# Storing three second-level factors in the first group, and loading the quarters of the rest two sets ahead

## The chip, the cores and the metric

The kernel runs on one core of a Trainium2 chip. The metric is the device time of one execution in microseconds; lower is better. Several runs are taken and the median is used. The profile comes from one further execution, of which a trace of every instruction was kept; its time is given beside its span (first to last instruction).

## What is computed

An attention with a decaying state, over 12 blocks of 64 tokens, feeds a two-layer map with the activation h - tanh(h):

```python
B, H, S, D = (4, 8, 768, 64)
for b in range(nb):                       # blocks of 64 tokens
    intra = einsum('bhic,bhjc->bhij', qb, kb) * Dmask
    out[:, :, sl] = einsum('bhij,bhjd->bhid', intra, vb) + einsum('bhid,bhde->bhie', qb * lam_pow, kv_state)
    kv_state = lam_block * kv_state + einsum('bhsd,bhse->bhde', kb * rev_pow, vb)
x = out.transpose(0, 2, 1, 3).reshape(3072, 512)
h = x @ w_in                              # w_in  512 x 2048
return (h - tanh(h)) @ w_out              # w_out 2048 x 512
```

All arithmetic is in 32-bit floats, and the result is 3072 x 512.

## The kernel before

**Groups.** The tokens are worked off in six groups (`g` = 0 to 5) of 512 rows: 128 positions of each of the four batches. For each group the attention gives x transposed (`xt`), the "up" product makes the hidden values g, and the "down" product makes the output.

**Group 0** is computed plainly (`up_plain`, `down_plain`), while the weights come in. Each raw block is rounded (`round_block`: ACT L239 and L241, VectorE L242 to L248). `down_plain(kt)` goes through the eight row blocks `kt` of w_out. For each of them `sums_out(kt)` forms, from the four blocks B11, B12, B21, B22 of w_out, the sums T1, T2, T4, T3 of a Strassen-Winograd product (L221 to L224), and stores the seven factors B11, B21, B22, T1, T2, T4, T3 into the DRAM tensor `factors` (L226, L227, issued by POOL). The weight tile `wt` (pool `wst`, two buffers) is filled again two `kt` later, by L241 first. Quarter `kt // 2` and row half `kt % 2` say where a row block belongs at the second level.

**Groups 1 to 5** use the seven products instead of eight, in both layers. `up(g, u, n)` is product n of column block u; its four accumulation banks are y (two, by the parity of u), z and w. z takes the products 5, 7 and 3, so product 5 of the next u can overwrite it only after VectorE has read it for product 3 (L419), and product 3 only after it has been read for product 7 (L414). In `down`, products 1 and 2 are done at one level (L501), products 4, 5, 6, 7 and 3 at two levels (`down_twice`, L539): each is again split in seven, and for this each of the five factors needs seven second-level factors, in the DRAM tensor `fine`: its blocks b11, b21, b22 and the sums t1, t2, t3, t4 of its four quarters.

**How `fine` is made.** This is done in group 1, in five turns among the 28 products of "up". `load_quarters(n)` loads the four quarters of one factor from `factors` (L444: 256 KB each, in pieces of 512 bytes), and `factors_twice(n)` forms four sums on VectorE (L459) and stores seven tiles to `fine` (L461). `turns` gives the count of products after which each turn comes. The quarters live in the ring `wb` of seven buffers, which the factor blocks of "down" use too (`piece`, L470 and L473, up to seven blocks ahead). The sums live in four buffers with the tag `sums`, three of them used by a turn.

**The order of work.** The instructions of each engine are put in order by a planner, in which what is ready first, and then what is written first, goes first; a sum marked `keep_in_program_order` stays behind what was written before it on its engine. Each engine then runs its instructions strictly in that order. Almost all transfers that concern weights, factors and outputs are issued by POOL; the loads of q, k and v are issued by SP, among them the small block loads of groups 2 to 5 (16 KB each, L136). Pools `qpool`, `wst` and `stage` are closed after group 0, and the pool `late` (ring `wb`, `sums`) takes their memory. Pool `o` has four buffers, for outputs: `ob` of group 0 (L601, stored at L602), later the products of "down".

Of the kernel before, what the change touches and what calls it, by code (L numbers as in the profile page):

```python
# [9 lines left out]
F32 = mybir.dt.float32  # L10
# [13 lines left out]
def kernel(  # L24
# [31 lines left out]
    nc = tc.nc  # L56
# [8 lines left out]
    NU = DFF // 512  # L65
# [11 lines left out]
    opool = ctx.enter_context(tc.tile_pool(name="opool", bufs=4))  # L77
# [6 lines left out]
    dram = ctx.enter_context(tc.tile_pool(name="dram", bufs=1, space=bass.MemoryType.DRAM))  # L84
# [32 lines left out]
    raw, late = {}, {}  # L117
# [49 lines left out]

    NX = 7
    factors = dram.tile([NX, 128, KH, 256], F32, name="factors")
    w_in_u = moe_w_in.rearrange("k (a n) -> k a n", a=2)  # L170
    blocks = [("in", u, i) for u in range(NU) for i in range(KI)] + [("out", kt, a) for kt in range(KH)
                                                                    for a in range(2)]
# [45 lines left out]
    def sums_out(kt):  # L218
        wt = pair[kt]
        b11, b12, b21, b22, t1, t2, t4, t3 = (wt[:, x] for x in range(8))  # L220
        nc.vector.tensor_tensor(t1, b12, b11, op=AL.subtract)  # L221
        nc.vector.tensor_tensor(t2, b22, t1, op=AL.subtract)
        nc.vector.tensor_tensor(t3, b22, b12, op=AL.subtract)
        nc.vector.tensor_tensor(t4, b21, t2, op=AL.subtract)  # L224
        f = factors[:].rearrange("x p k c -> p x k c")
        nc.gpsimd.dma_start(out=f[:, 0:1, kt, :], in_=wt[:, 0:1, :])  # L226
        nc.gpsimd.dma_start(out=f[:, 1:NX, kt, :], in_=wt[:, 2:8, :])  # L227

    def round_block(w, raw64):


        word = raw64.rearrange("p a n -> p (a n)").bitcast(U32).rearrange("p (n w) -> p n w", w=2)
        wordf = raw64.rearrange("p a n -> p (a n)").bitcast(F32).rearrange("p (n w) -> p n w", w=2)
        lo, hi = word[:, :, 0], word[:, :, 1]
        w = w.rearrange("p a n -> p (a n)")
        wb, wi = w.bitcast(U32), w.bitcast(I32)

        r = stage.tile([128, 512], I32, name="r", tag="r", bufs=2)
        nc.scalar.activation(r, lo, AF.Copy, scale=2.0 ** -29)  # L239

        nc.scalar.activation(w, wordf[:, :, 1], AF.Abs)  # L241
        nc.vector.tensor_scalar(out=w, in0=w, scalar1=CLAMP, scalar2=None, op0=AL.max)  # L242

        nc.vector.tensor_scalar(out=wb, in0=wb, scalar1=3, scalar2=0x3FFFFFF8, op0=AL.logical_shift_left,
                                op1=AL.bitwise_and)
        nc.vector.scalar_tensor_tensor(out=wb, in0=hi, scalar=0xC0000000, in1=wb, op0=AL.bitwise_and,
                                       op1=AL.bitwise_or)
        nc.vector.tensor_tensor(wi, wi, r, op=AL.add)  # L248
# [109 lines left out]
    def attention(g):  # L358
        pieces = [[(fn, g, bs) for fn in (att_transpose, att_scores, att_out, att_state)] for bs in ((0, 1), (2, 3))]
        pieces[1].append((att_sums, g, None))  # L360
        return pieces


    FACT = {1: ("A11", "B11"), 2: ("A12", "B21"), 3: ("S4", "B22"), 4: ("A22", "T4"), 5: ("S1", "T1"),
            6: ("S2", "T2"), 7: ("S3", "T3")}
    XAT = {"B11": 0, "B21": 1, "B22": 2, "T1": 3, "T2": 4, "T4": 5, "T3": 6}
# [57 lines left out]

    SUB = (1, 2, 6, 5, 7, 3, 4)
    TWICE = (4, 5, 6, 7, 3)

    fine = dram.tile([len(TWICE), len(SUB), 128, NU, 128], F32, name="fine")  # L430
    HIDAT = {"A11": 11, "A12": 21, "A22": 22, "S1": "S1", "S2": 11, "S3": 12, "S4": 21}
    RING = 7

    def twice(g, n):
        return n in TWICE and not (g == NG - 1 and n == 3)

    stream = [(g, n, x) for g in range(1, NG) for n in (1, 2, 4, 5, 6, 7, 3)
              for x in (SUB if twice(g, n) else range(NU))]
    sent = {"n": 0}

    def factor_block(t, x, i, j):

        src = factors[x].rearrange("p (u m) c -> p u m c", m=2)
        nc.gpsimd.dma_start(out=t, in_=src[:, :, i, ts(j, 128)])  # L444

    quarters = {}

    def load_quarters(n):
        for i in range(2):
            for j in range(2):  # L450
                quarters[n, i, j] = late["pool"].tile([128, NU, 128], F32, name="wq", tag="wb", bufs=RING)
                factor_block(quarters[n, i, j], XAT[FACT[n][1]], i, j)

    def factors_twice(n):

        b11, b12, b21, b22 = (quarters.pop((n, i, j)) for i in range(2) for j in range(2))
        t1, t2, t4 = (late["pool"].tile([128, NU, 128], F32, name=f"wt{x}", tag="sums", bufs=4) for x in (1, 2, 4))
        for dst, x, y in ((t1, b12, b11), (t2, b22, t1), (b12, b22, b12), (t4, b21, t2)):
            tc.keep_in_program_order(nc.vector.tensor_tensor(dst, x, y, op=AL.subtract))  # L459
        for i, t in enumerate((b11, b21, t2, t1, b12, b22, t4)):  # L460
            nc.gpsimd.dma_start(out=fine[TWICE.index(n), i], in_=t)  # L461

    def piece(g, n, x):

        i = stream.index((g, n, x))
        while sent["n"] < min(i + RING, len(stream)):
            g_, n_, x_ = stream[sent["n"]]
            t = late["pool"].tile([128, 2, 256], F32, name="wb", tag="wb", bufs=RING)
            if twice(g_, n_):
                nc.gpsimd.dma_start(out=t.rearrange("p m c -> p (m c)"),  # L470
                                    in_=fine[TWICE.index(n_), SUB.index(x_)].rearrange("p u c -> p (u c)"))
            else:
# [20 lines left out]
    def down(g, n):  # L493

        t, first = product_bank(("down", g), n)
        a = hidden(g, HIDAT[FACT[n][0]])
        for u in range(NU):
            wb = piece(g, n, u)
            for m in range(2):
                for kt in range(2):  # L500
                    nc.tensor.matmul(out=t[:, m, :], lhsT=a[:, u, kt, ts(m, 128)], rhs=wb[:, kt, :],  # L501
                                     start=first and u == 0 and m == 0 and kt == 0, stop=u == NU - 1 and kt == 1,
                                     skip_group_check=True)
        t = t.rearrange("q m c -> q (m c)")
        if n == 1:
            res[g, 1] = otile("q1")
            nc.scalar.activation(res[g, 1], t, AF.Copy)
        else:
            o11 = late["pool"].tile([128, 512], F32, name="o11", tag="o11", bufs=1)
            nc.vector.tensor_tensor(o11, res[g, 1], t, op=AL.add)  # L510
            store(g, 11, o11)
            sums_once(g, 11, "S1", 11)
# [6 lines left out]
    def sums_twice(g, n):  # L519
        a11, a12, a21, a22 = quarter(g, n)  # L520
        s1, s2 = (late["pool"].tile([128, NU, 128], F32, name=f"s{x}", tag="sums", bufs=4) for x in (1, 2))
        nc.vector.tensor_tensor(s1, a21, a22, op=AL.add)
        nc.vector.tensor_tensor(s2, s1, a11, op=AL.subtract)
        nc.vector.tensor_tensor(a21, a11, a21, op=AL.subtract)
        low[g, n] = (s1, s2)
# [79 lines left out]
    def run(pieces):  # L605
        for fn, *args in pieces:
            fn(*args)
# [31 lines left out]
    early.close()  # L639
    late["pool"] = ctx.enter_context(tc.tile_pool(name="late", bufs=1))  # L640

    turns, made = (4, 9, 14, 19, 23), []
    load_quarters(TWICE[0])
    up(1, 0, 1)
    for g in range(1, NG):
        last = g == NG - 1
        p0, p1 = attention(g + 1) if not last else ([], [])
        for u in range(NU):
            for n in (2, 6, 5, 7, 1, 4, 3):
                if n != 1:  # L650
                    up(g, u, n)
                elif u + 1 < NU:
                    up(g, u + 1, 1)
                else:
                    down(g, 1)
                if g == 1:
                    made.append(n)
                    if len(made) in turns:
                        t = turns.index(len(made))
                        factors_twice(TWICE[t])  # L660
                        if t + 1 < len(TWICE):
                            load_quarters(TWICE[t + 1])
            if not last and u > 1:
                run(p0[u - 2:u - 1])
        sums_twice(g, 4)
        down(g, 2)
        run(p0[2:])
        sums_twice(g, 5)
        down_twice(g, 4, "z")
        run(p1[0:1])  # L670
        sums_once(g, 21, 21, 11)
        sums_twice(g, 6)
        down_twice(g, 5, "w")
        run(p1[1:2])
        sums_twice(g, 7)
        down_twice(g, 6, "z")
        if not last:
            sums_twice(g, 3)
        run(p1[2:])
        down_twice(g, 7, "w")  # L680
        if not last:
            up(g + 1, 0, 1)
            down_twice(g, 3, "z")
        else:
            down_end(g)
# [30 lines left out]
```

## Time and profile before

| | |
|---|---|
| three runs | 697.58, 697.76, 699.11 us; median 697.76 |
| the profiled execution | 696.26 us, span 694.5 us |
| instructions | 12442 |
| mean granted TensorE clock | 0.990 |
| DMA | 123.27 MB, mean 177 GB/s |
| POOL's queue (q0) | 91.77 MB, 40.8% of 16 engines' span |
| SP's queue (q1) | 30.71 MB, 22.8% |
| quarters loaded (L444) | 20 of 256 KB, 759 ns of POOL each, 5.6 us to landing |
| second-level factors stored (L461) | 20 quarters and 15 sums of 256 KB, 540 to 557 ns of POOL each |
| sums of quarters (L459) | 20 of 0.68 us |

Parts of the span, from the starts of TensorE's instructions: down_plain from 83.7 to 154.6 us; "up" of group 1 from 154.6; `down(1, 1)` at 215.4; the two-level products of group 1 from 241.1; the last matmuls end at 691.7. A busy time is the time in which an engine was at work, and DMA share is the mean busy share of the 16 DMA engines. In the timeline and the waits, what stands after the arrow is what the waiting instruction was released by.

### The profile page before, as it was taken

What the parts mean: (1) busy time and instruction counts of PE and PEld (TensorE: products, weight loads), DVE (VectorE), ACT (ScalarE), POOL (GpSimd) and SP (SyncE); (2) the same over time, 40 slices, a digit from 0 to 9 for tenths busy, and PEclk for the clock granted to TensorE, in tenths of its full rate; (3) what the DMA queues carried; (4) which work ended last, traced back from release to release, by engine and by line L of the source; (5) the groups of instructions that cost most, each with busy time, mean ns of one, the idle gap of its engine ahead of it and who ended that gap; (6) DMA issues with size and microseconds to landing.
All of it is one profiled execution on the core that took longest, in us unless ns stands there. A gap on an engine that the chain in (4) does not pass through costs nothing.

```text
span 694.5 us, 12442 instructions
## 1 busy us (share of the span) xinstructions
PE 669.3 (96%) x4688; PEld 578.5 (83%) x4688; DVE 449.1 (65%) x786; ACT 195.0 (28%) x392; POOL 184.9 (27%) x328
## 2 busy tenths in 40 slices
PE   6899999999796999999999999999999999999998
PEld 5688855558575899988899988899888899988898
DVE  3797766995366886347787356778346786345653
ACT  2664433323120112232112233122233122233120
POOL 0001212124664244100244200243400144400262
PEclk9999999999898999999999999999999999999999
DMA  9879868468988798544598820687820376600385
GB/s 190 217 215 228 278 174 261 143 156 255 286 261 245 216 273 242 161 82 84 134 266 243 227 54 14 136 247 217 254 46 2 90 214 211 214 1 0 96 289 178
DMA packets 160475, 123.27 MB, mean 177 GB/s; under 512 B 133536, under 2 KB 133920, under 8 KB 160416
## 3 DMA queue, kind: packets, MB, share of 16 engines
q0 software_dynamic: 27552, 91.77, 40.8%
q1 hardware_dynamic: 132720, 30.71, 22.8%
q8 instruction: 37, 0.61, 0.4%
q14 instruction: 22, 0.18, 0.1%
q10 hardware_dynamic: 144, 0.00, 0.0%
HBM read 99.62 MB, written 22.81 MB: 176 GB/s over the span
## 4 chain that ended last, share of the span: by engine, by line
PE 79%; DMA 9%; issue 7%; POOL 3%; DVE 1%; ACT 1%; SPq 0%; POOLq 0%
PE y L393 16%; PE y L539 11%; PE zw L539 8%; PE z L393 8%; PE h L581 8%; PE y L501 5%; PE w L501 5%; DMA wq<-factors 4%; PE op L597 4%; PE w L393 4%; PE sp L291 3%; PE op L342 2%; DMA wb<-fine 2%; DMA raw<-in_moe_w_in_dram 1%; PE op L336 1%
## 5 line engine op out<-in xcount | busy, mean ns | idle before, releaser
L470 POOL DMA_DIRECT2D wb<-fine x168 | 90.3, 538 | 141.7 <-PE y L539 55.5
L473 POOL DMA_DIRECT2D wb<-factors x44 | 23.9, 544 | 187.1 <-PE y L501 176.9
L393 PE MATMUL y<-xt,w 128*128 128x256 f32 x320 | 73.2, 380 | 0.0
L393 PEld LDWEIGHTS y<-xt,w 128*128 128x128 f32 x320 | 60.5, 190 | 8.6 <-issue 0.5
L401 ACT ACTIVATE th<-g 128x512 f32<-128x512 f32 x60 | 37.7, 630 | 99.6 <-DVE g L419 42.9
L539 PE MATMUL y<-wb,g 128*128 128x128 f32 x456 | 61.3, 278 | 0.3 <-ACT r L542 0.3
L542 ACT ACTIVATE q<-y 128x128 f32<-128x128 f32 x96 | 26.6, 277 | 121.2 <-PE y L539 120.3
L402 DVE TENSOR_TENSOR g<-g,th 128x512 f32<-128x512 f32 x60 | 41.4, 690 | 27.9 <-ACT th L401 27.7
L539 PEld LDWEIGHTS y<-wb,g 128*128 128x128 f32 x456 | 55.7, 192 | 2.0 <-issue 0.8
L597 PE MATMUL op<-wt,g 128*128 128x512 f32 x128 | 56.5, 596 | 0.0
L581 PE MATMUL h<-xt,w 128*128 128x256 f32 x256 | 56.1, 381 | 0.0
L581 PEld LDWEIGHTS h<-xt,w 128*128 128x128 f32 x256 | 48.4, 190 | 7.2 <-issue 0.3
L597 PEld LDWEIGHTS op<-wt,g 128*128 128x128 f32 x128 | 23.9, 190 | 27.7 <-issue 27.0
L393 PE MATMUL z<-xt,ws 128*128 128x256 f32 x160 | 39.7, 393 | 4.6 <-DVE g L414 4.6
L501 PE MATMUL y<-wb,g 128*128 128x256 f32 x160 | 37.4, 393 | 6.4 <-DMA fine<-wq 6.4
L414 DVE TENSOR_TENSOR g<-g,z 128x512 f32<-128x512 f32 x20 | 13.7, 686 | 45.2 <-ACT g L413 45.2
L501 PEld LDWEIGHTS y<-wb,g 128*128 128x128 f32 x160 | 31.4, 197 | 11.2 <-issue 6.8
L539 PE MATMUL zw<-wb,g 128*128 128x128 f32 x304 | 40.2, 276 | 0.0
L393 PEld LDWEIGHTS z<-xt,ws 128*128 128x128 f32 x160 | 31.4, 197 | 9.5 <-DVE g L414 5.0
L393 PE MATMUL z<-tt,ws 128*128 128x256 f32 x160 | 37.9, 380 | 1.4 <-DVE g L419 1.4
L393 PE MATMUL w<-xt,w 128*128 128x256 f32 x160 | 38.8, 387 | 0.0
L393 PE MATMUL y<-tt,w 128*128 128x256 f32 x160 | 38.4, 382 | 0.0
(119 smaller groups left out, 1222.9 us busy)
## 6 DMA issues: line engine op xcount, KB each, us to landing
wb<-fine POOLq DMA_DIRECT2D x168, 256.0 KB, 3.9
wb<-factors POOLq DMA_DIRECT2D x44, 256.0 KB, 5.1
raw<-in_moe_w_out_dram POOLq DMA_DIRECT2D x16, 512.0 KB, 4.9
v_nat<-in_v_dram SPq DMA_DIRECT2D x24, 256.0 KB, 5.1
factors<-wt POOLq DMA_DIRECT2D x8, 768.0 KB, 5.5
k_nat<-in_k_dram SPq DMA_DIRECT2D x20, 256.0 KB, 5.4
wq<-factors POOLq DMA_DIRECT2D x20, 256.0 KB, 5.6
fine<-wq POOLq DMA_DIRECT2D x20, 256.0 KB, 4.0
```

The source lines that it names most:

```text
L291: nc.tensor.matmul(out=sp[j][:, p, :], lhsT=kt[ts(j, 64), p, :], rhs=qt[ts(j, 64), p, :], start=True, stop=True)
L342: nc.tensor.matmul(out=dst(n, p, j), lhsT=vn[:, 2 * p + j, :], rhs=ss[:, j, p, :], start=g == 0 and n == 0 and p % 2 == 0, stop=n == 1 and ...
L393: nc.tensor.matmul(out=t[:, m, :], lhsT=wt[:, kt, ts(m, 128)], rhs=x[:, kt, :], start=first and m == 0 and kt == 0, stop=kt == 1, skip_gro ...
L401: nc.scalar.activation(th, src, AF.Tanh)
L402: nc.vector.tensor_tensor(dst(c), src, th, op=AL.subtract)
L470: nc.gpsimd.dma_start(out=t.rearrange("p m c -> p (m c)"), in_=fine[TWICE.index(n_), SUB.index(x_)].rearrange("p u c -> p (u c)"))
L473: nc.gpsimd.dma_start(out=t, in_=factors[XAT[FACT[n_][1]]][:, 2 * x_:2 * x_ + 2, :])
L501: nc.tensor.matmul(out=t[:, m, :], lhsT=a[:, u, kt, ts(m, 128)], rhs=wb[:, kt, :], start=first and u == 0 and m == 0 and kt == 0, stop=u = ...
L539: nc.tensor.matmul(out=dst, lhsT=a[:, u, :], rhs=wb[:, ts(u, 128)], start=x in (1, 2) and u == 0, stop=u == NU - 1, skip_group_check=True)
L542: nc.scalar.activation(keep, dst, AF.Copy)
L581: nc.tensor.matmul(out=hm[:, m, :], lhsT=w1[u][:, i, a, ts(m, 128)], rhs=xt[0, t][:, i, :], start=m == 0 and i == 0, stop=i == KI - 1, ski ...
L597: nc.tensor.matmul(out=obank[b], lhsT=g, rhs=wt[:, 2 * a:2 * a + 2, :], start=kt == 0 and a == 0, stop=kt == KH - 1 and a == 1)
```

## The change

Three things change.

1. `fine` is created early, and `sums_out(kt)` stores into it too. What it stores are quarters that need no second-level sum: of each of B22, T1, T2, T4 and T3 the quarter b11 (even `kt`), or b21 and b22 (odd `kt`). One store writes the same quarter of five factors: 128 partitions, 5 factors, 128 numbers each.
2. `factors_twice` stores only the four sums t1, t2, t3 (in place of b12) and t4, no longer b11, b21, b22.
3. The sets of quarters are numbered 0 to 4 in the order `MADE` (factors 4, 5, 6, 7, 3). Even sets stay in the ring `wb`, odd sets go into the four buffers of pool `o`. Sets 0 and 1 are loaded at the start, and set t + 2 after turn t. The turns come after 6, 11, 15, 20 and 24 products in place of 4, 9, 14, 19 and 23.

```diff
+    SUB = (1, 2, 6, 5, 7, 3, 4)
+    TWICE = (3, 5, 6, 4, 7)
+    fine = dram.tile([len(TWICE), len(SUB), 128, NU, 128], F32, name="fine")
...
         nc.gpsimd.dma_start(out=f[:, 0:1, kt, :], in_=wt[:, 0:1, :])
         nc.gpsimd.dma_start(out=f[:, 1:NX, kt, :], in_=wt[:, 2:8, :])
+
+        for x, j in ((1, 0),) if kt % 2 == 0 else ((2, 0), (3, 1)):
+            nc.gpsimd.dma_start(out=fine[:, SUB.index(x), :, kt // 2, :].rearrange("n p c -> p n c"),
+                                in_=wt[:, 3:8, ts(j, 128)])
...
-    def factor_block(t, x, i, j):
-
-        src = factors[x].rearrange("p (u m) c -> p u m c", m=2)
-        nc.gpsimd.dma_start(out=t, in_=src[:, :, i, ts(j, 128)])
-
+    MADE = (4, 5, 6, 7, 3)
     quarters = {}

-    def load_quarters(n):
+    def load_quarters(t):
+        src = factors[XAT[FACT[MADE[t]][1]]].rearrange("p (u m) c -> p u m c", m=2)
         for i in range(2):
             for j in range(2):
-                quarters[n, i, j] = late["pool"].tile([128, NU, 128], F32, name="wq", tag="wb", bufs=RING)
-                factor_block(quarters[n, i, j], XAT[FACT[n][1]], i, j)
-
-    def factors_twice(n):
-
-        b11, b12, b21, b22 = (quarters.pop((n, i, j)) for i in range(2) for j in range(2))
+                if t % 2 == 0:
+                    x = late["pool"].tile([128, NU, 128], F32, name="wq", tag="wb", bufs=RING)
+                else:
+                    x = opool.tile([128, NU, 128], F32, name="oq", tag="o")
+                nc.gpsimd.dma_start(out=x, in_=src[:, :, i, ts(j, 128)])
+                quarters[t, i, j] = x
+
+    def factors_twice(t):
+
+        b11, b12, b21, b22 = (quarters.pop((t, i, j)) for i in range(2) for j in range(2))
         t1, t2, t4 = (late["pool"].tile([128, NU, 128], F32, name=f"wt{x}", tag="sums", bufs=4) for x in (1, 2, 4))
         for dst, x, y in ((t1, b12, b11), (t2, b22, t1), (b12, b22, b12), (t4, b21, t2)):
             tc.keep_in_program_order(nc.vector.tensor_tensor(dst, x, y, op=AL.subtract))
-        for i, t in enumerate((b11, b21, t2, t1, b12, b22, t4)):
-            nc.gpsimd.dma_start(out=fine[TWICE.index(n), i], in_=t)
+        for x, src in ((5, t1), (6, t2), (7, b12), (4, t4)):
+            nc.gpsimd.dma_start(out=fine[TWICE.index(MADE[t]), SUB.index(x)], in_=src)
...
-    turns, made = (4, 9, 14, 19, 23), []
-    load_quarters(TWICE[0])
+    turns, made = (6, 11, 15, 20, 24), []
+    load_quarters(0)
+    load_quarters(1)
...
-                        factors_twice(TWICE[t])
-                        if t + 1 < len(TWICE):
-                            load_quarters(TWICE[t + 1])
+                        factors_twice(t)
+                        if t + 2 < len(MADE):
+                            load_quarters(t + 2)
```

More of the change, by code (lines that the diff above doesn't have):

```diff
@@ L423, in up @@
             nc.vector.tensor_tensor(dst(12), dst(11), dst(12), op=AL.subtract)
-    SUB = (1, 2, 6, 5, 7, 3, 4)
-    TWICE = (4, 5, 6, 7, 3)
-    fine = dram.tile([len(TWICE), len(SUB), 128, NU, 128], F32, name="fine")
     HIDAT = {"A11": 11, "A12": 21, "A22": 22, "S1": "S1", "S2": 11, "S3": 12, "S4": 21}
```

## The prediction

> **What bounds the kernel now.** I read the page's parts 1 and 2 first:
>
> ```profile
> PE 669.3 (96%) x4688; PEld 578.5 (83%) x4688; DVE 449.1 (65%) x786; ACT 195.0 (28%) x392; POOL 184.9 (27%) x328
> PEclk9999999999898999999999999999999999999999
> DMA  9879868468988798544598820687820376600385
> ```
>
> TensorE is busy for 96% of the span, so time can only come from its idle stretches or from slow matmuls. PEclk dips in slices 10 and 12 (about 174 and 208 us), the stretch in which group 1 makes its second-level factors. Next, the waits of TensorE alone; of its nine rows these belong to that stretch:
>
> ```profile
> PE y L501 <- DMA fine<-wq: 6.4, 1, 6.4
> ...
> PE z L393 <- DVE g L414: 4.6, 1, 4.6
> ...
> PE z L393 <- DVE g L419: 1.4, 1, 1.4
> ```
>
> They are 12.4 of the 22.3 us that the nine rows add up to. Then the timeline around them (start, length, engine, line, what it waited for):
>
> ```profile
> 181.00 0.69 DVE L459 TENSOR_TENSOR wt<-wq,wt 128x512 f32<-128x512 f32 x1 [6.85 <-DMA wq<-factors]
> ...
> 182.81 0.68 DVE L414 TENSOR_TENSOR g<-g,z 128x512 f32<-128x512 f32 x1
> ...
> 183.55 3.78 PE L393 MATMUL z<-xt,ws 128*128 128x256 f32 x8 [4.63 <-DVE g L414]
> ...
> 189.84 1.89 PE L393 MATMUL y<-tt,ws 128*128 128x256 f32 x8
> ...
> 209.31 0.55 POOL L473 DMA_DIRECT2D wb<-factors  x1 [0.42 <-DMA wq<-factors]
> ...
> 215.44 3.75 PE L501 MATMUL y<-wb,g 128*128 128x256 f32 x8 [6.39 <-DMA fine<-wq]
> ```
>
> A sum of quarters (L459) stands on VectorE until a quarter has landed; L414, which reads PSUM bank z, is queued behind it, and TensorE can't overwrite z. Later the first factor block of down(1,1) is issued only at 209.31, behind the last loads and stores of quarters. And eight matmuls after such a wait take 3.78 us instead of 1.89. The table by stretch (us, busy times, granted clock, DMA share, GB/s) says why, and how full the DMA engines are:
>
> ```profile
> 139.00:156.00 17.00, 17.00 (x89) 9.13 (x84) 15.86 (x30) 3.47 (x6) 4.05 (x6) 1.00 0.63 155
> 183.00:196.00 13.00, 12.45 (x45) 10.50 (x46) 8.40 (x14) 4.05 (x7) 7.32 (x12) 0.76 0.97 287
> 209.00:222.00 13.00, 6.61 (x21) 5.40 (x21) 8.11 (x14) 1.23 (x2) 5.21 (x10) 0.74 0.82 227
> ```
>
> **What the Trainium skill says.** "TensorE: Matmul & The Clock Gate", Part 1: after an idle window of about 3.4 us the array's clock is halved until it has been busy as long. The trace agrees: after 4.63 and 6.39 us idle the granted clock is 0.76 and 0.74, after 1.44 us the eight matmuls take 1.99 us. "DMA: Bandwidth & Descriptors", Specifications: full rate needs pieces of 512 B. The new stores and the quarter loads have just that; in 158 to 170 us, mostly quarter loads, the queue of POOL moves 2.65 MB in 12 us at 69.1% share, 320 GB/s per full share, and in 575 to 592, only 2 KB pieces, 3.51 MB in 17 us at 65.4%, 316. So 512 B cost nothing extra. The same page, Queues, rings and completion order: queues share the 16 engines in turn. In 183 to 196 the small block loads of SP take 17.1% and POOL's queue 79.6%.
>
> **What can be won.** TensorE's starts give it. Idle: 4.63 + 1.44 + 6.39 + 0.26 (before the block at 250.56) = 12.7 us. Slow restarts, by start-to-start against 1.73 for eight: 183.55 to 187.12 is 3.57 (+1.84), to 189.84 another 2.72 (+0.99), 205.26 to 209.05 +0.2, 215.44 to 218.99 is 3.55 (+1.82): 4.85. Together 17.5 us, all of it charged to the making of these factors.
>
> **The change, part by part.**
> - *Twelve stores more in the first group* (even kt one, odd two; 320 KB in 640 pieces). On POOL 512 pieces take 0.76 us (L444), 768 take 0.85 (L227): about 0.8 each, 9.6 us. They stand behind L227 of each kt, ahead of the next raw load (L179) or L226. POOL waits there for VectorE anyway: 2.24, 2.48, 6.14, 2.92 and 2.70 us after kt 2 to 6, so 0.8 or 1.6 fits. They hold the weight tile, whose next writer is L241 on ACT. From L227 to the L241 that refills the tile there are 9.0 us at worst (81.75 to 90.74, 99.34 to 108.40, 127.93 to 136.99); a store lands 2.5 + 5.1 = 7.6 us after L227 starts, up to 10.8 with the longest landing of the trace (8.3). Behind L241 are the other ACT work and the chain to L248, ready at 144.3 for a matmul at 147.75: 3.4 us of cover more. Cost 0; without the covers some 1.7 us each. DMA share there is 0.45 to 0.88; 3.93 MB at 320 GB/s are 12.3 us spread over 70.
> - *Fifteen stores less in group 1* (L461, three per turn): 8.4 us of POOL, as many bytes off the stretch at 0.82 to 0.97 share. They also freed late: a quarter's slot now opens with the sum that last reads it, except b12.
> - *Two sets ahead, odd sets in pool o.* A set is issued one turn before it is needed today, 6 to 8 us landing included; later, it has two turns, some 15 us. Set 1 goes where the outputs ob lie: their stores were issued by 159.2 and land in 4.3, so that set is issued by about 164 and is needed at about 178. For sets 2 to 4 the same count leaves 3 to 6 us.
> - *Turns at 6, 11, 15, 20, 24*: same 20 sums of 0.6 us. A product takes 1.73 us, so without waits turn k falls at 154.6 + 1.73 (k + 1): 166.7, 175.4, 182.3, 190.9, 197.8, and down(1,1) starts at 199.5 rather than 215.4.
> - *Queued behind a late sum*: on VectorE, L419 or L414 that free bank z; TensorE's next product in z stands behind them.
>
> **What remains.** (1) Turn 0: the stores of kt 7 (two, to 155.2) lie ahead of set 0 in the queue, and the late pool takes the memory of the weight tiles, so set 0 may have to wait for them. Set 0's last quarter landed near 166.3; 0.66 MB at 262 GB/s (80% of 325) is 2.5 us, the landing wait up to 2.2. So 168.5 to 171; three sums after it, then L419 by 171 to 173.6; TensorE wants z at 171.85. 0 to 1.7, I take 0.9. (2) down(1,1): from 152.7 POOL's queue must move before the first block: f 0.79, its two stores 0.66, ob 1.05, quarters 5.24, stores of four turns 4.19, the block 0.26: 12.2 MB, at 262 GB/s 46.5 us, to 199.2, needed at 199.5. The fourth block waits for turn 4's first sum, near 200 to 201. 0 to 2 us, I take 1.0. (3) Other short waits, 0 to 1: 0.4. Sum 2.3, none over 3.4 us, so no restart. Gain 17.5 - 2.3 = 15.2. The profiled execution (696.26, span 694.5 and 1.76 around it) becomes 681.1; the median of the runs is 1.5 above it, so 697.76 - 15.2 = 682.6.
>
> **Rivals.**
> - *The wait moves to the DMA engines.* POOL's queue got 2.65 MB in 12 us in one stretch (221 GB/s), 3.11 in 13 (239) in another: 12.2 MB then take 51 to 55 us, and down(1,1) waits 4 to 8 us with a restart of 1.8. For it: the shares of 0.9. Against it: those rates had POOL waiting in between. Won 17.5 - 8 to 10: 688 to 690. Chance 0.20.
> - *Turn 0 and its restart.* Set 0 held behind ob and the kt 7 stores for 4 us more: VectorE's queue stops, TensorE stands 4 to 5 us and restarts slowly (2.8): 17.5 - 7.5 - 1.4: about 689. Against it: ob's stores were in the queue before too. Chance 0.12.
> - *Slower: the buffers of the sums.* A turn takes three of four `sums` tiles, so its second sum waits for the store of the last turn's first to land. Turns lie 6.9 us apart once waits are gone, and stores queue behind up to eight loads (2.1 MB, 8 us). Bank z gives 1.7 us more. Up to 8.6 us of landing nothing is lost; each us above costs TensorE one at four turns. It takes (17.5 / 4) + 8.6 = 13 us to be slower; the longest landing seen is 8.3. With 14 to 15 us: 702 to 707. Chance 0.12.
> - *The change doesn't do what it says*: the planner issues the second set no earlier, or down's blocks still behind the last stores: 6.4 + 1.8 stay, and some of turn 1: near 697. Chance 0.04.
>
> **The numbers.** Forecast 682.6, chance 0.52, own range 680 to 686 (all of (1) to (3) at zero or at their most: 680.3 to 685.0). The two middle rivals reach 690, plus 2.5 for both in part: 679.8 to 692.5 leaves out the slower case, no change and a little more. Within 0.2% (1.4 us) is about what can't be told from no change. Faster 0.84 (0.52 + 0.20 + 0.12), same 0.03, slower 0.13.
>
> **What would show it.** Right: the rows of TensorE waiting for DMA and for L414 gone or under 2 us; PEclk without dips; down(1,1) starting near 200; turns at the times above; fine<-wq and fine<-oq together five, and twelve 320 KB stores to `fine` before 156 us, with L597 unbroken. Wrong: a new TensorE wait over 3.4 us in 154 to 225, ACT L241 waiting for a store, or VectorE's sums waiting for a store's landing.

## The result, and the profile after

The changed kernel takes 697.4 us (median of four runs, 696.2 to 698.1) where the kernel before takes 697.9 in the same comparison: a ratio of 0.9988, 95% interval 0.9970 to 1.0006. That is no difference. The forecast was 682.6. The profiled execution (697.4 us) has a span of 695.6 us, 1.1 more than before.

In the changed kernel the line numbers are some five to eight higher: L401 is the "up" product (before L393), L506 and L544 the "down" products (L501, L539), L464 the sums of quarters (L459), L279 the transposes of the q and k blocks (L271). L136, the block loads of SP, kept its number.

Rows of the page's part 2, after (the slices count from 0):

```profile
PE   6999999999979869999999999999999999999998
...
PEclk9999999999998979999999999999999999999999
DMA  9879869669967848544598740588820366600385
```

The clock's dip in slice 10 is gone. It dips in slices 12 and 14 now (209 to 226 and 243 to 261 us), and TensorE's busy share falls in 11, 13 and 14. The waits of TensorE in the changed kernel (total, times, longest):

```profile
PE zw L544 <- issue: 8.5, 1, 8.5
PE y L506 <- DVE g L410: 5.5, 1, 5.5
```

All three waits that the prediction set out to remove are gone: the two for L414 and L419, and the one ahead of down(1,1). Two new ones, of 14.0 us together, have come. TensorE's timeline in that stretch:

```profile
198.52 5.34 PE L506 MATMUL y<-wb,g 128*128 128x256 f32 x24
209.38 3.78 PE L506 MATMUL y<-wb,g 128*128 128x256 f32 x8 [5.51 <-DVE g L410]
...
249.66 2.04 PE L544 MATMUL zw<-wb,gS 128*128 128x128 f32 x8 [8.52 <-issue]
...
256.27 1.16 PE L544 MATMUL y<-wb,g 128*128 128x128 f32 x8
```

and the last of these products in the kernel before:

```profile
256.31 1.16 PE L539 MATMUL y<-wb,g 128*128 128x128 f32 x8
```

Down(1,1) starts at 198.52, where it started at 215.44, so 16.9 us had been won by then. At 230.16 the two-level products start, 10.9 us earlier than before. By 256.3 nothing of this is left: the product that starts there, at 256.27, started at 256.31 in the kernel before. VectorE's timeline names what it waited for:

```profile
198.71 0.70 DVE L279 STREAM_TRANSPOSE qt<-q_blk 128x512 f32<-128x512 f32 x1
207.43 0.71 DVE L279 STREAM_TRANSPOSE kt<-k_blk 128x512 f32<-128x512 f32 x1 [8.03 <-DMA q_blk<-in_q_dram]
...
247.68 0.71 DVE L279 STREAM_TRANSPOSE kt<-k_blk 128x512 f32<-128x512 f32 x1 [6.78 <-DMA k_blk<-in_k_dram]
```

Both waits are for k block tiles of the attention of group 2, loaded by SP. (The row at 207.43 names q_blk, but what the transpose reads is the k tile loaded just before it, issued until 205.92.) Behind the first stands L410, which the last quarter of down(1,1) needs; behind the second stands L549 (before L544), the subtraction that a product on bank zw needs. SP's queue in the changed kernel (start, length of 16 issues):

```profile
163.08 9.57 SPq L136 DMA_DIRECT2D q_blk<-in_q_dram  x16
...
196.67 9.25 SPq L136 DMA_DIRECT2D k_blk<-in_k_dram  x16
...
236.19 10.06 SPq L136 DMA_DIRECT2D k_blk<-in_k_dram  x16
```

and in the kernel before, with VectorE's last transpose of group 2:

```profile
157.10 10.11 SPq L136 DMA_DIRECT2D q_blk<-in_q_dram  x16
...
188.11 9.96 SPq L136 DMA_DIRECT2D k_blk<-in_k_dram  x16
...
233.00 8.23 SPq L136 DMA_DIRECT2D k_blk<-in_k_dram  x16
```
```profile
249.56 0.67 DVE L271 STREAM_TRANSPOSE kt<-k_blk 128x512 f32<-128x512 f32 x1
```

What SP waited for ahead of its first block load, before and then after, tells why the chain starts when it does (`wt` is the weight tile):

```profile
SPq L136 <- DVE wt L224: 6.8, 1, 6.8
SPq L136 <- DMA factors<-wt: 4.6, 1, 4.6
```
```profile
SPq L136 <- DMA factors<-wt: 10.1, 1, 10.1
SPq L136 <- DMA fine<-wt: 6.6, 2, 3.9
```

Before, it starts when the last store to `factors` has read the weight tile; after, the new stores to `fine` come last.

The reader should see a second chain beside the first one. The eight block tiles of group 2 are 128 loads on SP, issued one after the other, which takes 83 to 84 us in both kernels. Before, the fourth tile was out at 198.1 and VectorE took it at 210.9; the eighth was out at 241.2 and was taken at 249.6. The last three loads of these tiles landed at most 3.2 and 2.3 us after the start of their issue, so by about 200.8 and 243.1. That leaves some 10 and 6.5 us of slack, no more. After, this chain starts 6.0 us later, and TensorE arrives 11 to 17 us earlier.

The sum of TensorE's losses between "up" and 256 us then comes out nearly the same. After: 5.51 + 8.52 us idle and 5.3 us of slow matmuls behind these waits (209.38 to 215.39: 6.01 for sixteen of them where 3.46 is usual; 249.66 to 256.27: 6.6 where the kernel before took 3.9), 19.3 in all. Before it was 17.5, and group 0 ended 1.1 us later, 18.6 together; the two agree within 1 us.

### The profile page after: what moved, and what is told of

Same layout as the page of the kernel before. It is cut to its first block, busy times and chain, and to the rows that moved or that the text cites. A ratio compares the mean times of both kernels' runs of the same rounds, so it can differ in the third digit from the quotient of the medians.

```text
span 695.6 us, 12454 instructions
## 1 busy us (share of the span) xinstructions
PE 669.5 (96%) x4688; PEld 579.4 (83%) x4688; DVE 450.0 (65%) x786; ACT 194.7 (28%) x392; POOL 188.0 (27%) x325
## 4 chain that ended last, share of the span: by engine, by line
PE 79%; DMA 8%; issue 5%; SPq 2%; DVE 2%; POOL 2%; ACT 0%; POOLq 0%; DVEq 0%
PE y L401 16%; PE y L544 11%; PE z L401 8%; PE h L586 8%; PE zw L544 8%; PE w L506 5%; PE op L602 5%; PE y L506 5%; PE w L401 4%; PE sp L299 3%; DMA q_blk<-in_q_dram 3%; SPq L136 2%; PE op L350 2%; DMA wb<-fine 2%; PE tp L284 1%
## 5 line engine op out<-in xcount | busy, mean ns | idle before, releaser
L401 PE MATMUL y<-xt,w 128*128 128x256 f32 x320 | 73.2, 379 | 0.0
L401 PEld LDWEIGHTS y<-xt,w 128*128 128x128 f32 x320 | 60.5, 190 | 8.5 <-issue 0.5
L544 PE MATMUL y<-wb,g 128*128 128x128 f32 x456 | 61.3, 278 | 0.0
L410 DVE TENSOR_TENSOR g<-g,th 128x512 f32<-128x512 f32 x60 | 41.4, 689 | 27.5 <-ACT th L409 27.2
L544 PEld LDWEIGHTS y<-wb,g 128*128 128x128 f32 x456 | 55.7, 192 | 1.5 <-issue 0.3
L602 PE MATMUL op<-wt,g 128*128 128x512 f32 x128 | 56.5, 595 | 0.0
L602 PEld LDWEIGHTS op<-wt,g 128*128 128x128 f32 x128 | 23.8, 190 | 27.7 <-issue 26.5
L506 PE MATMUL y<-wb,g 128*128 128x256 f32 x160 | 37.4, 393 | 5.5 <-DVE g L410 5.5
L544 PE MATMUL zw<-wb,g 128*128 128x128 f32 x304 | 40.2, 275 | 0.0
L506 PEld LDWEIGHTS y<-wb,g 128*128 128x128 f32 x160 | 31.4, 197 | 10.4 <-DVE g L410 5.9
L303 DVE TENSOR_TENSOR ss<-sp,mask 128x512 f32<-128x512 f32 x48 | 30.8, 682 | 13.3 <-PE sp L299 13.3
L401 PE MATMUL y<-tt,w 128*128 128x256 f32 x160 | 38.6, 385 | 0.0
L401 PE MATMUL w<-xt,w 128*128 128x256 f32 x160 | 37.8, 379 | 0.0
L401 PE MATMUL y<-tt,ws 128*128 128x256 f32 x160 | 37.8, 379 | 0.0
L401 PE MATMUL z<-tt,ws 128*128 128x256 f32 x160 | 37.8, 379 | 0.0
```

The source lines that it names most:

```text
L303: nc.vector.tensor_tensor(ss[:, j], sp[j], mask[:, j], op=AL.mult)
L401: nc.tensor.matmul(out=t[:, m, :], lhsT=wt[:, kt, ts(m, 128)], rhs=x[:, kt, :], start=first and m == 0 and kt == 0, stop=kt == 1, skip_gro ...
L410: nc.vector.tensor_tensor(dst(c), src, th, op=AL.subtract)
L544: nc.tensor.matmul(out=dst, lhsT=a[:, u, :], rhs=wb[:, ts(u, 128)], start=x in (1, 2) and u == 0, stop=u == NU - 1, skip_group_check=True)
L602: nc.tensor.matmul(out=obank[b], lhsT=g, rhs=wt[:, 2 * a:2 * a + 2, :], start=kt == 0 and a == 0, stop=kt == KH - 1 and a == 1)
```

## The experiments

Theory S: SP's chain of block loads sets the end of group 1; it starts when the memory of the weight tiles has been read for the last time (the block tiles lie in the pool `late`, on that memory), and the two stores of kt 7 delay this. Theory D: the DMA engines, busy 0.97 from 153 to 198 us, set it, and only bytes count. The kernel before was run again beside them, and scatters more there: from 693.9 to 702.0 us over 69 runs in three comparisons, with medians of 698.2, 698.3 and 696.6. Each ratio is to the kernel before of the same comparison; most of the kernels below have four runs, and a range behind a ratio is its 95% interval.

### The two parts alone

`stores_only` keeps the first-group stores and the four stores of a turn, with the loading and turns of before:

```diff
+        for x, j in ((1, 0),) if kt % 2 == 0 else ((2, 0), (3, 1)):
+            nc.gpsimd.dma_start(out=fine[:, SUB.index(x), :, kt // 2, :].rearrange("n p c -> p n c"), in_=wt[:, 3:8, ts(j, 128)])
...
-        for i, t in enumerate((b11, b21, t2, t1, b12, b22, t4)):
-            nc.gpsimd.dma_start(out=fine[TWICE.index(n), i], in_=t)
+        for x, src in ((5, t1), (6, t2), (7, b12), (4, t4)):
+            nc.gpsimd.dma_start(out=fine[TWICE.index(n), SUB.index(x)], in_=src)
```

> The first-group stores alone: `fine` gets its three quarters per factor in group 0, a turn stores four tiles; quarters one set ahead, turns 4, 9, 14, 19, 23 and the ring as before. Theory S (SP's block loads for group 2, which can start only when the memory of the weight tiles has been read for the last time, and which take some 83 us for eight tiles, set the end of group 1): the loads start near 163 as in the changed kernel, the eighth tile lands near 247, and the time stays within 3 us of the kernel before, 695 to 700. Theory D (the DMA engines, busy 0.97 from 153 to 198, set it): fifteen stores less in the stretch shorten the chain of quarters, 690 to 693.

`ahead_only` is the changed kernel without the first-group stores and with all seven stores in each turn:

```diff
-        for x, j in ((1, 0),) if kt % 2 == 0 else ((2, 0), (3, 1)):
-            nc.gpsimd.dma_start(...)
...
-        for x, src in ((5, t1), (6, t2), (7, b12), (4, t4)):
+        for x, src in ((1, b11), (2, b21), (6, t2), (5, t1), (7, b12), (3, b22), (4, t4)):
```

> The loading two sets ahead alone, with the turns at 6, 11, 15, 20, 24, seven stores per turn, none in group 0. Theory S: the block loads start near 157 again, 6 us earlier than in the changed kernel, so both waits end some 4 to 6 us earlier: 691 to 694. Theory D: 3.9 MB more in the stretch at a share of 0.97, 12 us at 320 GB/s: 700 or more.

Measured: `stores_only` 697.0, ratio 0.9987 (0.9972 to 1.0002); `ahead_only` 696.5, ratio 0.9976 (0.9952 to 0.9999), with nineteen of its twenty runs between 691.4 and 701.1. In the medians neither part alone brings more than a quarter of a per cent. SP's first block loads, of `stores_only` and then of `ahead_only`:

```profile
162.88 9.03 SPq L136 DMA_DIRECT2D q_blk<-in_q_dram  x16
```
```profile
156.74 10.94 SPq L136 DMA_DIRECT2D q_blk<-in_q_dram  x16
```

With the stores the chain starts at 163, without them at 157, as S says. In `stores_only` TensorE has the same wait as in the changed kernel, 9.0 us ahead of a zw product, with VectorE waiting 15.8 us for k blocks. So theory D's 690 to 693 didn't come, though fifteen stores had left the stretch. `ahead_only` missed both forecasts in its median. Its profiled execution (692.6) is one of its fastest; VectorE waits there for no block load longer than 1.9 us, and TensorE waits 6.6 us for factor blocks of down(1,1). Why most of its runs are slower stays open.

### Without the two stores of kt 7

```diff
-        for x, j in ((1, 0),) if kt % 2 == 0 else ((2, 0), (3, 1)):
+        for x, j in () if kt == KH - 1 else ((1, 0),) if kt % 2 == 0 else ((2, 0), (3, 1)):
...
+        for x, src in ((2, b21), (3, b22)):
+            nc.gpsimd.dma_start(out=fine[TWICE.index(MADE[t]), SUB.index(x), :, NU - 1, :], in_=src[:, NU - 1, :])
```

> The changed kernel, but without the two stores of the last row block kt 7, which stand just ahead of the end of group 0; their part (the last of four column blocks of b21 and b22) is stored by each turn from the quarter tiles, ten small stores of 64 KB. Theory S: block loads start near 157 to 159 in place of 163.1, time 691 to 694. Theory D: the same bytes in the stretch, 697.

Measured: 689.7, ratio 0.9892 (0.9851 to 0.9933). The start of SP's chain:

```profile
159.17 10.95 SPq L136 DMA_DIRECT2D q_blk<-in_q_dram  x16
```

It starts 3.9 us earlier than in the changed kernel, and VectorE has no wait for a block any more. The same bytes are moved and the time fell all the same, so D is wrong about this. S gave the direction, but its 691 to 694 was missed too, by 1.3 us. (The profiled execution is the slowest of the four, 694.6; the others took 688.9 to 690.3.) That VectorE doesn't wait is in part because it comes later: it takes the fourth tile at 210.6 and the eighth at 246.4, about as in the kernel before, since TensorE loses 7.6 us to factor blocks and 2.8 us to bank z. These are the edit's own cost, of which below; so this trace doesn't show by itself where the gain comes from.

### The block tiles off the memory of the weight tiles

The block tiles get a pool of their own, on the memory of the rounding buffers, which are read for the last time near 144 us:

```diff
-    stage = early.enter_context(tc.tile_pool(name="stage", bufs=1))
+    stage = early.enter_context(tc.tile_pool(name="stage", bufs=1, side="right"))
...
+    late["blk"] = ctx.enter_context(tc.tile_pool(name="blk", bufs=1, side="right"))
...
-                x = late["pool"].tile([128, NP, BLK // 32, 32], F32, name=f"{name}_blk", tag="blk", bufs=2 * B - 1)
+                x = late["blk"].tile([128, NP, BLK // 32, 32], F32, name=f"{name}_blk", tag="blk", bufs=2 * B - 1)
```

> The changed kernel with the seven block tiles in a pool of their own, laid over the memory of the rounding buffers (last read near 144) and not of the weight tiles. Theory S: the block loads start near 145, 18 us earlier, and both waits on VectorE (8.0 and 8.7 us) go; with the waits of TensorE of 5.5 and 8.5 us and the slow matmuls after them some 17 to 19 us: 678 to 682. Theory D: nothing is moved off the DMA engines, at most 2 us: 695 to 698.

Measured: 692.8, ratio 0.9914 (0.9880 to 0.9947), between the two forecasts. The chain starts at 144.68, and the two waits shrank from 5.5 and 8.5 us to none and 2.0. But a new one had come, as TensorE's timeline shows, and SP's queue says why:

```profile
259.44 1.13 PE L319 MATMUL kv<-v_nat,k_nat 128*64 128x64 f32 x16 [5.43 <-DVE k_nat L314]
```
```profile
233.44 12.00 SPq L136 DMA_DIRECT2D q_blk<-in_q_dram  x16
245.53 9.93 SPq L136 DMA_DIRECT2D k_blk<-in_k_dram  x15
255.57 0.39 SPq L126 DMA_DIRECT2D k_nat<-in_k_dram  x1
```

The k tile of a batch of group 2 has to wait for one of three buffers, and the planner has put 31 block loads of group 3 ahead of it in SP's queue. TensorE, 12.6 us ahead of the kernel before at the second scores (241.7 against 254.3), runs into this.

### A fourth k buffer

```diff
+                if name == "k" and g >= GB and b == B - 1:
+                    x = late["blk"].tile([128, H, D], F32, name="k_nat", tag="k3", bufs=1)
+                else:
+                    x = (qpool if name == "q" else io).tile([128, H, D], F32, name=f"{name}_nat", tag=name, bufs=bufs)
```

> blk_own_after with a fourth buffer for the k tile of batch 3, so that its load doesn't stand behind 31 block loads of group 3 in SP's queue. Theory S: the wait of TensorE for k_nat (5.4 us, and about 2 us of slow matmuls) goes, nothing else: 684 to 687 where blk_own_after had 692.8. Theory D: the wait turns up somewhere else again, 690 to 693.

Measured: 683.3, ratio 0.9793 (0.9744 to 0.9843), 15 us faster than before. The four runs go from 681.2 to 688.9; the profiled one took 682.0. The page and the waits of TensorE in the stretch:

```profile
span 680.3 us, 12461 instructions
...
PEclk9999999999999999999999999999999999999999
```
```profile
PE zw L547 <- issue: 3.4, 1, 3.4
...
PE y L509 <- DMA wb<-factors: 0.8, 1, 0.8
```

In the median this is the time that was forecast for the change alone. What is left, 3.4 us, is again VectorE standing at the transpose of the last k tile (4.6 us, until 237.85): SP's chain ends at 233.1 here, after 88 us. The wait's row names the v tile issued right behind it, but that one landed 7.1 us after 233.1, at 240.2, too late to have been it. The last k block landed 6.0 us after the start of its issue at 231.5, at about 237.5.

The same edits, put on the kernel before, are the control:

> The kernel before with the block tiles in a pool of their own over the rounding buffers, and a fourth buffer for the k tile of batch 3 (groups 2 to 5). Theory S: the kernel before wasn't bound by SP's block loads (they were there 10 and 7 us before VectorE took them) but by the waits of its turns; an earlier start brings nothing: within 2 us of before. Theory M (the move of the block loads is what helps, whatever the factors do): 6 us faster, as blk_own_after was.

Measured: 697.2, ratio 0.9981 (0.9967 to 0.9996), so 1.2 us in the median and 2.3 us at most. TensorE's waits there:

```profile
PE y L504 <- DMA fine<-wq: 6.2, 1, 6.2
PE z L396 <- DVE g L417: 6.0, 1, 6.0
...
PE z L396 <- DVE g L422: 1.1, 1, 1.1
```

They are the waits of the turns, as before. So the two limits stand one behind the other. In the medians, taking away either brings 0.1 to 0.2%, taking away both 2.1%. (The changed kernel doesn't take away the first alone: it also starts SP's chain 6 us later.)

### The kt 7 stores and the first-group stores, with SP out of the way

`blk_own_k4_kt7` joins `blk_own_k4` with the edit of kt 7 shown above, `ahead_only_own_k4` joins it with that of `ahead_only`.

> The same, and the two stores of row block kt 7 replaced by ten small ones in the turns. Theory S: the block loads no longer hang on these stores, so it is worth only what set 0 of the quarters gains (it waited until 164.8): 0 to 2 us against blk_own_k4. Theory D: the same bytes, no difference.

> Two sets ahead without the first-group stores (seven stores per turn), with the block tiles of their own and the fourth k buffer. It prices the stores once SP's loads are out of the way. Theory S with the DMA engines as the next limit: 3.9 MB more in the stretch from 154 to 200, some 4 to 8 us of new waits for factor blocks: 688 to 693, slower than blk_own_k4. If the stores are worth nothing: as blk_own_k4.

Measured: 688.8, ratio 0.9858 (0.9833 to 0.9882), and 691.9, ratio 0.9907 (0.9879 to 0.9935). The first missed both forecasts: its median is 5.5 us above that of `blk_own_k4` (four runs from 688.3 to 689.0, where three of that kernel's four took 681.2 to 684.6 and the fourth 688.9). POOL's queue in it shows the reason:

```profile
187.97 0.56 POOL L471 DMA_DIRECT2D fine<-wq  x1 [3.98 <-DMA wq<-factors]
...
198.76 0.56 POOL L471 DMA_DIRECT2D fine<-oq  x1 [3.94 <-DMA oq<-factors]
...
202.72 1.08 POOL L483 DMA_DIRECT2D wb<-factors  x2
```

A store of a quarter as it was loaded needs no sum, so the planner puts it right behind its load, and POOL stands until the quarter has landed. The first factor blocks of down(1,1) went out at 202.7, where they went out at 191.4 in `blk_own_k4`, and TensorE waits 5.9 us for them. The same rows (L461, waiting for L444's loads) were in the kernel before, 21.9 us of them in eleven waits. The second kernel prices the first-group stores once nothing hides them: 691.9 against 683.3, 8.6 us. It came out as its first forecast had it, 688 to 693, though not by the DMA engines alone: POOL stands behind loads there too (4.16 us ahead of the store at 202.77), and VectorE waits 3.3 us for a store of the sums. How much each of these is worth was not separated.

### Half of the chain on ACT

In `act_k` the changed kernel keeps its memory, and the k blocks of group 2 are issued by ACT; in `act_k_own_k4` this is put on `blk_own_k4`.

```diff
-                        nc.sync.dma_start(out=x[ts(c, 32), p], in_=...)
+                        (nc.scalar if name == "k" and g == GB else nc.sync).dma_start(out=x[ts(c, 32), p], in_=...)
```

> The changed kernel with the memory as it is, but the 64 block loads of k of group 2 issued by ACT and not by SP: the start near 163 stays, the eight tiles come in two queues of four. Theory S, in its form that the length of SP's chain counts as much as its start: the q tiles are done near 205 in place of 246, both waits of VectorE for blocks go; ACT pays 64 issues of 0.45 us, and its first one stands until 163 ahead of a copy that TensorE needs, 3 to 5 us: 684 to 690. If only the start counts: 697.

> blk_own_k4 with the k blocks of group 2 on ACT. In blk_own_k4 the last tile of SP's chain (issued until 233) still kept VectorE 4.6 us and TensorE 3.4 us. Theory S: this goes too, 679 to 682. Against it: ACT's issues push back its copies and tanh, 683 to 687.

Measured: 714.1, ratio 1.0251 (1.0195 to 1.0307), and 708.7, ratio 1.0163 (1.0124 to 1.0202). All the forecasts were too low. VectorE had no wait for a block, but TensorE waits for ACT (of `act_k`):

```profile
PE y L402 <- ACT g L422: 12.7, 4, 5.4
PE y L402 <- ACT g L420: 8.7, 3, 4.4
```
```profile
164.97 7.56 ACTq L136 DMA_DIRECT2D k_blk<-in_k_dram  x7
172.58 0.60 ACT L422 ACTIVATE g<-y 128x512 f32<-128x512 f32 x1 [7.03 <-DMA k_blk<-in_k_dram]
```

Seven issues held ACT for 7.56 us, not the 3.2 that was counted at 0.45 each, with a copy that frees a PSUM bank behind them. So whether a shorter chain with the late start would have done is not settled by these runs.

## Why the prediction was wrong

**What can be won.** The working was right as a sum: 17.5 us lost to idle stretches and slow restarts. The step that failed is the one after it, "all of it charged to the making of these factors". Those waits were only the first of two limits. In the kernel before SP's chain had 10 and 6.5 us of slack in the same stretch, less than the 17.5 us to be won, and the change itself made the chain start 6.0 us later. By an estimate from these two figures about half a microsecond was left to win; the prediction listed SP's share of the DMA engines, but never laid SP's queue beside the new times.

**The stores of the first group.** "Cost 0" was right for group 0: the copy that refills a weight tile (now L249) waits for TensorE six times and never for a store, and L602 runs unbroken. The prediction asked for "the next writer" of the weight tile and named L241. For kt 7 there is none; what comes next on that memory is the pool `late`. It saw this for set 0 of the quarters, gave it up to 2.2 us, and missed that SP's block tiles lie in the same pool. The last of the stores is issued from 156.47 to 157.33 and lands 6.5 us after 156.47, near 163, and that is when both start: 163.08 for SP, 6.0 us after the 157.10 of before, and 163.60 for POOL:

```profile
163.60 2.96 POOL L456 DMA_DIRECT2D wq<-factors  x4 [3.67 <-DMA fine<-wt]
```

**Two sets ahead, turns, down(1,1).** Right in the main. The sums of turns 0 to 3 begin at 168.4, 178.5, 185.6 and 191.4, which is 0.5 to 3.3 us after the forecast, and TensorE didn't wait for them; those of turn 4, forecast for 197.8, begin at 209.2, behind the first block wait. Down(1,1) was forecast for 199.5 and started at 198.5 with no wait for its block. The price of 0.9 us for turn 0 came out as no wait at all.

**What remains.** The terms (1) to (3), 2.3 us, were, if anything, too large: between 154 and 256 us TensorE waited for none of the factors. The rate behind (2), 262 GB/s, held: POOL's queue moved 12.16 MB from 153 to 198 us, 270 GB/s. The missing term was SP's, 14.0 us idle and 5.3 us of slow matmuls.

**Rivals.** The DMA engines as the new limit: their share was 0.97 from 153 to 198, and TensorE lost nothing there. Turn 0: POOL did stand until 163.6, at no cost. The buffers of the sums: no wait of VectorE for a store in the changed kernel (in the four kernels with six or seven stores a turn and two sets ahead there is one of 3.2 to 4.0 us). "The change doesn't do what it says" had 0.04 and the right time, but not the right reason: the change does all that it says. The case that came about, a second limit just behind the first, was none of the rivals. Nearly all the signs of being right came (the rows of waits gone, down(1,1) near 200, five stores of quarters left), and so did a sign of being wrong: a new wait over 3.4 us between 154 and 225, the one that ends at 209.4.

**The clock gate** (the Trainium skill, "TensorE: Matmul & The Clock Gate", Part 1: half the clock after some 3.4 us without work) was read rightly, and it counted twice: the new waits of 5.5 and 8.5 us brought their slow matmuls with them (granted clock 0.80 and 0.70 in the stretches 198 to 215 and 240 to 257), which used up what was left of the gain: the product that the second wait held starts 2.8 us earlier than in the kernel before (249.66 against 252.44), and the slow matmuls from there to 256.3 cost 2.7 us.

## What to carry to other kernels

Before pricing the removal of a wait, follow every other queue through the same stretch and write down when each thing lands and when it is taken; the least slack, less what the change delays that queue, is about what can be won. When memory changes hands between stages, a store added at the end of the first stage can be paid by whatever is allocated there next, on any queue, not only by the tile's own next writer. And a change that brings nothing may be half of one that brings 2%: try it again with the second limit lifted.

## What the runs showed that was not expected

- A store of data that needs no arithmetic can be dear: standing right behind its load in POOL's queue, it held POOL up to 4 us at a time, and ten small ones in place of two large ones cost 5.5 us in the median.
- The 16 issues of a block tile have no fixed length: in the changed kernel they take SP 7.7 us at a DMA share of 0.38 (205.97 to 213.64), 9.6 to 11.2 us at 0.94 and more (the first three tiles), and 14.5 us at 0.85 (213.68 to 228.22). The share alone doesn't give the length.
- The same issues on ACT took about 1.1 us each at 165 us (7.56 us for seven), with the copies and tanh behind them pushed back, and the kernel became 17 us slower than the kernel before.
